# An adaLN block with linear attention and a token mixer on one core: row turns in F32R, last channels of phi(q) in pairs of tiles, two folded vectors, and a reordered beginning

## The chip, the core and the metric

The kernel runs on one core of one Trainium2 chip. The metric is device time in microseconds (us). Most executions of this kernel lie within 0.04 us of each other: three runs gave 437.96, 437.97 and 438.0. Engine names are those of the profile: PE is TensorE's products, PEld its weight loads, DVE is VectorE, ACT is ScalarE, POOL is GpSimd, SP is SyncE, which issues most of the DMAs.

## The reference

One sequence of S = 2048 tokens with D = 448 channels, H = 16 heads of 28, F = 1792. All inputs are float32.

```python
mod = (_silu(c) @ w_mod).reshape(c.shape[0], 6, 1, -1)
sa, ca, ga, sb, cb, gb = ...
h = _layernorm(x) * (1 + ca) + sa
x = x + ga * _A_ref(h, A_wqkv, A_wo)
h = _layernorm(x) * (1 + cb) + sb
x = x + gb * _B_ref(h, B_w1, B_b1, B_w2, B_b2)
```

`_A_ref` is linear attention: q, k and v from one projection, phi(t) = (t + 1 where t > 0, else exp(t)) + 1e-6, kv = phi(k)^T v summed over the tokens, and the output is phi(q) kv divided by phi(q) . sum(phi(k)) + 1e-6, times wo. `_B_ref` mixes tokens: gelu(h^T w1 + b1) w2 + b2, for each channel.

## The kernel before

A token tile is 128 tokens; there are NT = 16. A product in full float32 is made of F32R products: a number is split into a high half (an ACT copy to F32R) and a low half (a DVE subtraction), and hi*hi + hi*lo + lo*hi are added in PSUM. `bank(...)` is one of eight PSUM banks, `slot` and `tslot` are SBUF buffers, `moving` an F32R buffer of 448 columns. The kernel sets its own order: each engine runs its instructions in the order in which the lines call them, and waits where an operand or a buffer is not ready.

The 448 channels are three chunks of 128 and a last one of 64. The 64 channels of the last chunk share one product: high half in 64 partitions, low half in the other 64.

**The beginning** (lines 150 to 178 and 531 to 645). The loads go out one behind the other on SP's queue: weights of k (`load_qkv(1)`), the columns of w_mod that give 1 + ca (`load_first(1, ch)`) and those that give sa (`load_first(0, ch)`), the transposed tokens `load_xt(t)` and the tokens `load_x(t)`. `keep_warm(n)` issues n float32 products of 128 columns, each as two instructions, whose result nobody reads. `col_sum(j, ch)` (L220) gives a chunk of the modulation as a column on DVE; `w_high`, `w_low` and `w_row` scale and split the weights; `row_part(1, ch)` (L265, L267) adds up sa times the weights into `accb`, which `row_bias` (L277) sums with a product; `row_sum` (L274) sums the weights' columns; `row_out` (L281, L282) turns both into rows of `Wrow`. `a_split_high(t)` (L398) and `a_split_low(t)` (L402) split tile t of xt. `projects` and `project` (L419) make x times the weights of k (`kp`) or q (`qp`), and `close` (L426) adds mean and bias as one more product, for which the tile's mean and root must stand as rows in its low half.

Each tile's statistics come from ACT for tiles 0 and 1 (`a_stats_act`, L348 to L356) and from DVE for the others (`a_stats_dve`, L367 to L373); the power -0.5 is on POOL (`a_pow`, L339). Two tiles' statistics are put in columns (`a_rows`, L382 and L385), turned by one PE instruction to rows (`a_transpose`, L391; eight in all), and copied by ACT (`a_copy`, L394). `a_exp` (L433, L436) and `a_pk` (L441) make phi(k); `a_pk_parts` (L499, L501 or L503 and a DMA that adds, L504) splits it and adds it to one of two running sums, for tiles 2 to 12 with a DMA on POOL's queue that adds (L508). `a_norm`, `a_high` and `a_low` (L479 to L489) make and split the normalised tile, and `a_outer` (L525, L529) adds the tile's phi(k) x^T.

**The k loop** (lines 647 to 736) does tiles 4 to 15, with five tiles of q in between. In it and behind it, `mod_part`, `mod_split` and `mod_sum2` (L226 to L241) make modulation vectors 2, 3, 4 and 5: four chunks of 112 rows are weighted and added on DVE, split, and summed over the partitions by two products with ones.

**The phi(q) loop** (lines 932 to 1001) is a pipeline of steps i over the tiles; LAG = 5. In PE's order a step has `b_transpose(i)` (L820, three transposes of 128 columns, and L821, one of 64), `b_out(i - 1)` (L845, eleven products), a tile of q in the first steps, and from step 5 on twelve products of the mixer's first matrix for tile i - 5 (`step`, L895 to L897). DVE's order within a step is: a part of vector 5 in steps 13 to 16 (L226, L228), `b_res(i - 2)` (L854, the residual, which reads the bank of `b_out(i - 2)`), `b_prod(i + 1)` (L795), `b_norm1_a` (L864), `b_sum(i + 1)` (L799), `b_norm1_b` (L868), `b_low(i)` (L830), `b_recip(i + 1)` (L805), `b_low_last(i)` (L834), `b_scale(i + 1)` (L809, which writes the `pn` that the next step's transposes turn), and `b_low2(i - 4)` (L892). ACT starts a step with `b_high(i)` (L825, L826).

Behind it, to the end, come the rest of the mixer's first matrix (L895 to L897) and its second (L1109 to L1113).

## Time and profile before

| What | us |
|---|---|
| Median of three runs | 437.97 |
| The profiled execution: device time | 438.01 |
| Its span, first to last instruction | 436.3 |
| PE busy within the span | 429.2 |
| PE's share of the chain that ended last | 89% |
| DVE busy | 360.6 |
| ACT busy | 275.3 |
| POOL busy | 117.9 |

A row of the timeline is: start in us, duration in us, engine, line of the kernel, operation, what it writes and reads, shape, count, and in brackets how long the engine was idle before it and what ended that. Two products in a row on PE overlap: each starts about 0.2 us behind the one before and takes 0.36 to its modelled end, so the distance of the starts is what a product costs. A row of busy time by stretches is: the stretch, its length, then busy time and count for PE, PEld, DVE, ACT and POOL, the granted clock of PE, the DMA engines' share and GB/s. A row of groups is: line, engine, operation, shapes, count, then busy us and mean ns of one, then idle us before them and what ended it.

### The profile page before, as it was taken

To read this page: it belongs to the slowest core of one execution; us is meant where nothing else is said; L and a number is where in the kernel's file an instruction comes from. 1 tells how busy PE (TensorE), PEld (TensorE's weight loads), DVE (VectorE), ACT (ScalarE), POOL (GpSimd) and SP (SyncE) were. 2 spreads that over 40 slices of the span, in tenths; PEclk is the share of its full clock that TensorE was granted. 3 is DMA by queue.
4 is the path that set the end of the run, shared out by engine and by line. 5 is a ranking of instruction groups with operands and counts; after the bars stand their busy time and mean duration, and the time that the engine had idled before them with its cause. 6 is when DMAs were issued, how large, how long until landed. Compare 5 with 4: busy or idle time off the path is not lost.

```text
span 436.3 us, 7203 instructions
## 1 busy us (share of the span) xinstructions
PE 429.2 (98%) x2337; PEld 398.8 (91%) x2337; DVE 360.6 (83%) x809; ACT 275.3 (63%) x587; POOL 117.9 (27%) x200
## 2 busy tenths in 40 slices
PE   8899999999999999999999999999999999999996
PEld 8688899999899999999999999999999999999996
DVE  4899986689799999994679695829799988898894
ACT  5689867749657798886756263537464565645550
POOL 4335454100024477773300000010113131132010
PEclk9999999999999999999999999999999999999999
DMA  8997998465300036335417561587379977985430
GB/s 273 382 338 154 228 230 200 80 193 180 124 2 0 26 66 152 74 74 139 152 65 223 178 209 45 148 213 218 71 171 235 201 173 156 223 180 119 83 54 32
DMA packets 63941, 66.14 MB, mean 152 GB/s; under 512 B 4960, under 2 KB 55456, under 8 KB 63904
## 3 DMA queue, kind: packets, MB, share of 16 engines
q1 hardware_dynamic: 54832, 50.90, 37.6%
q0 software_dynamic: 8784, 14.32, 20.9%
q10 hardware_dynamic: 288, 0.46, 0.5%
q8 instruction: 18, 0.29, 0.3%
q14 instruction: 19, 0.16, 0.1%
HBM read 46.30 MB, written 7.34 MB: 123 GB/s over the span
## 4 chain that ended last, share of the span: by engine, by line
PE 89%; DVE 3%; DMA 2%; ACT 2%; POOL 1%; issue 1%; SPq 1%; DVEq 0%; ACTq 0%; POOLq 0%
PE y L1112 19%; PE up L897 10%; PE up L896 10%; PE up L895 10%; PE y L1113 9%; PE op L845 8%; PE qp L419 7%; PE cacc L525 6%; PE kp L419 3%; PE tq L820 1%; DMA wr<-in_qkv_dram 1%; DMA x<-in_A_x_dram 1%; PE qp L426 1%; PE kvb L776 1%; DVE st L367 1%
## 5 line engine op out<-in xcount | busy, mean ns | idle before, releaser
L896 PE MATMUL up<-h2l,ph 128*128 128x448 f32 x224 | 81.3, 363 | 0.0
L897 PE MATMUL up<-h2h,pl 128*128 128x448 f32 x224 | 81.2, 363 | 0.0
L895 PE MATMUL up<-h2h,ph 128*128 128x448 f32 x224 | 80.8, 361 | 0.0
L1067 POOL DMA_DIRECT2D a<-a x16 | 14.2, 959 | 138.0 <-DMA a<-in_B_w_dram 77.1
L896 PEld LDWEIGHTS up<-h2l,ph 128*128 128x128 f32 x224 | 42.0, 188 | 3.3 <-DVE h2l L892 0.3
L895 PEld LDWEIGHTS up<-h2h,ph 128*128 128x128 f32 x224 | 41.9, 187 | 3.0
L897 PEld LDWEIGHTS up<-h2h,pl 128*128 128x128 f32 x224 | 42.0, 188 | 2.5
L84 DVE TENSOR_TENSOR pl<-pr,ph 128x512 fp32r<-128x512 f32 x46 | 30.7, 685 | 4.2 <-ACT ph L83 3.3
L1118 ACT ACTIVATE cc<-y 128x448 f32<-128x448 f32 x24 | 13.0, 547 | 26.8 <-PE y L1113 26.8
L83 ACT ACTIVATE ph<-pr 128x512 fp32r<-128x512 f32 x46 | 27.6, 625 | 0.8 <-PE up L897 0.5
L1031 DVE TENSOR_TENSOR u<-u,mod 128x448 f32<-128x448 f32 x14 | 8.7, 621 | 21.6 <-ACT u L1030 21.4
L419 PE MATMUL kp<-wh,hh 128*128 128x448 f32 x64 | 24.4, 386 | 0.2 <-ACT rk L436 0.2
L845 PE MATMUL op<-wph,pth 128*128 128x448 f32 x64 | 24.5, 383 | 0.0
L1030 ACT ACTIVATE u<-up,b1c 128x448 f32<-128x448 f32 x14 | 8.8, 627 | 24.0 <-PE up L897 23.5
L1132 POOL DMA_DIRECT2D out_dram<-yt x14 | 12.7, 910 | 40.5 <-DVE yt L1123 31.1
L525 PE MATMUL cacc<-pkh,xh 128*128 128x448 f32 x64 | 23.6, 369 | 0.0
L419 PE MATMUL qp<-wh,hh 128*128 128x448 f32 x64 | 23.4, 366 | 0.0
L845 PE MATMUL op<-wpl,pth 128*128 128x448 f32 x64 | 23.1, 361 | 0.0
L802 POOL TENSOR_SCALAR den<-den 128x16 f32<-128x16 f32 x16 | 8.8, 549 | 43.6 <-DVE den L799 43.6
L525 PE MATMUL cacc<-pkl,xh 128*128 128x448 f32 x56 | 20.3, 362 | 0.0
L1073 DVE TENSOR_TENSOR a<-a,s 128x512 f32<-128x512 f32 (+1 forms) x32 | 18.5, 619 | 0.0
L1112 PE MATMUL y<-ub,a11h 128*128 128x448 f32 x56 | 18.2, 375 | 0.0
(233 smaller groups left out, 1362.3 us busy)
## 6 DMA issues: line engine op xcount, KB each, us to landing
pr<-in_B_w_dram SPq DMA_DIRECT2D x56, 256.0 KB, 3.0
a<-in_B_w_dram SPq DMA_DIRECT2D x32, 256.0 KB, 4.6
a<-in_B_w_dram SPq DMA_DIRECT2D x32, 192.0 KB, 4.6
xt<-in_xt_dram SPq DMA_DIRECT2D x16, 256.0 KB, 5.0
x<-in_A_x_dram SPq DMA_DIRECT2D x16, 224.0 KB, 5.0
wm<-in_B_wmod_dram SPq DMA_DIRECT2D x16, 196.0 KB, 4.9
out_dram<-x SPq DMA_DIRECT2D x14, 224.0 KB, 2.4
out_dram<-yt POOLq DMA_DIRECT2D x14, 224.0 KB, 5.5
```

The costliest lines, as they stand in the source:

```text
L83: nc.scalar.activation(hi, full, AF.Copy)
L84: nc.vector.tensor_sub(lo, full, hi.bitcast(F32))
L419: nc.tensor.matmul(pps[t, j][:, :D], a[:, ch * P:(ch + 1) * P], w, start=first, stop=False)
L525: nc.tensor.matmul(cacc[ch][:, :D], a[:, s], b, start=(t == 0 and i == 0), stop=(t == NT - 1 and i == len(todo) - 1))
L845: nc.tensor.matmul(opb[t][:, :D], a, b, start=(n == 0), stop=(n == len(todo) - 1))
L895: nc.tensor.matmul(ps[:, :D], hi[:, sl], mh, start=first, stop=False)
L896: nc.tensor.matmul(ps[:, :D], hi[:, sl], ml, start=False, stop=False)
L897: nc.tensor.matmul(ps[:, :D], lo[:, sl], mh, start=False, stop=last)
L1067: nc.gpsimd.dma_start(w, a, accum_op=ALU.add)
L1073: nc.vector.tensor_tensor(w, raw2[q, a][i], raw2[q, b][i], op=op)
L1112: nc.tensor.matmul(ps[:, :D], h[:, s], w, start=opens and r == 0, stop=False, skip_group_check=True)
L1113: nc.tensor.matmul(ps[:, :HD], l[:, s], wh, start=False, stop=closes and r == PAIRS - 1, skip_group_check=True)
```

## The change

Five parts. (1) `ident_r` is an F32R copy of the identity; `a_transpose` multiplies by it in F32R instead of a float32 transpose. (2) `mod_split` of vectors 2 and 5 (`FOLDED`) adds rows 64 to 111 to rows 0 to 47 on DVE, puts high and low halves into one buffer of 128 partitions, and `mod_sum2` sums these with one product. (3) In the phi(q) loop an even tile's last 64 channels are copied by ACT (`b_beside`) into the columns behind the next, odd tile's channels, and the odd tile's fourth transpose turns both; `b_high` and `b_low_last` do the last channels of both tiles in the odd step, and an even tile's last two products (`b_out_last`) move to the start of PE's step i + 2, ahead of `b_transpose`; `b_res` of that tile keeps its place. (4) The sums of phi(k) by DMA are gathered and issued behind the power of the next statistics (`sum_end`). (5) The beginning is reordered: x0 ahead of the four `load_first(0, ch)` and x1 in their middle; seven instead of four `keep_warm`; `col_sum(0, .)` and `row_part(1, .)` alternate in twos; the splits of tiles 3 to 6 move; two small operations of `a_stats_act` go from POOL to DVE.

```diff
--- before.py
+++ after.py
@@ -42,6 +42,7 @@
 WARM = 6
 POOL_LOW = (0, 2)
 PRE = 9
+FOLDED = (2, 5,)
 MID = 5
 NSLOT, NTOK = 74, 27
 LOAD2, SPLIT2 = 12, 4
@@ -97,6 +98,7 @@
                             pattern=[[0, 4], [-DH, 4], [0, DH]], channel_multiplier=1)
     nc.gpsimd.affine_select(out=m3, in_=m3, compare_op=ALU.is_ge, fill=0.0, base=DH - 1,
                             pattern=[[0, 4], [DH, 4], [0, DH]], channel_multiplier=-1)
+    ident_r = cst.tile([P, P], F32R, name="ident_r")
     cst.tile([P, 112], F32, name="space")
     mhalf = cst.tile([P, 2], F32, name="mhalf")
     nc.vector.memset(mhalf, -0.5)
@@ -158,10 +160,11 @@
         if ch == 1:
             load_xt(1)
     load_xt(2)
+    load_x(0)
     for ch in range(4):
+        if ch == 2:
+            load_x(1)
         load_first(0, ch)
-    load_x(0)
-    load_x(1)
     load_xt(3)
     load_xt(4)
     load_x(2)
@@ -228,16 +231,31 @@
             nc.vector.scalar_tensor_tensor(macc[j], wm[j, k], sc[:G, k:k + 1], macc[j], op0=ALU.mult, op1=ALU.add)
 
 
+    def halves(acc, new, name):
+        n = acc.shape[0] - 64
+        nc.vector.tensor_add(acc[:n], acc[:n], acc[64:])
+        both = moving(new, name)
+        nc.scalar.activation(both[:64], acc[:64], AF.Copy)
+
+        def low():
+            nc.vector.tensor_sub(both[64:], acc[:64], both[:64].bitcast(F32))
+        return both, low
+
     def mod_split(j):
         acc = macc.pop(j)
-        macc[j] = (moving(slot, f"mh{j}", parts=G), moving(slot, f"ml{j}", parts=G))
-        split(acc, *macc[j])
+        if j in FOLDED:
+            both, low = halves(acc, slot, f"mh{j}")
+            low()
+            macc[j] = (both,)
+        else:
+            macc[j] = (moving(slot, f"mh{j}", parts=G), moving(slot, f"ml{j}", parts=G))
+            split(acc, *macc[j])
 
     def mod_sum2(j):
         ps = bank(f"modp{j}")
-        hi, lo = macc.pop(j)
-        nc.tensor.matmul(ps[:, :D], ones_r[:G, :], hi, start=True, stop=False)
-        nc.tensor.matmul(ps[:, :D], ones_r[:G, :], lo, start=False, stop=True)
+        part = macc.pop(j)
+        for i, m in enumerate(part):
+            nc.tensor.matmul(ps[:, :D], ones_r[:m.shape[0], :], m, start=(i == 0), stop=(i == len(part) - 1))
         return ps
 
     Whi, Wlo, Wrow, rowb, accb = {}, {}, {}, {}, {}
@@ -350,8 +368,8 @@
             b_square(X[t], s3[:, 1:2], s3[:, 2:3], f"s{t}")
 
         def end():
-            nc.gpsimd.tensor_scalar_mul(g[:, :, 0:1], sm[:, :, 0:1], 1.0 / D)
-            nc.gpsimd.tensor_scalar(ve, sm[:, :, 2:3].to_broadcast([P, n, 2]), 1.0 / D, EPS,
+            nc.vector.tensor_scalar_mul(g[:, :, 0:1], sm[:, :, 0:1], 1.0 / D)
+            nc.vector.tensor_scalar(ve, sm[:, :, 2:3].to_broadcast([P, n, 2]), 1.0 / D, EPS,
                                     op0=ALU.mult, op1=ALU.add)
             a_pow(g, ve)
             groups[ts[0]] = g
@@ -388,7 +406,7 @@
     def a_transpose(t):
         ps = bank(f"rw{t}")
         tps[t], tps[t + 1] = ps[:ROWS - 64, :P], ps[64:ROWS, :P]
-        nc.tensor.transpose(ps[:ROWS, :P], rowst[t // 2 % RING][:, :ROWS].bitcast(F32), ident)
+        nc.tensor.matmul(ps[:ROWS, :P], rowst[t // 2 % RING][:, :ROWS], ident_r, start=True, stop=True)
 
     def a_copy(t):
         nc.scalar.activation(heads[t][1][64:ROWS, 384:], tps.pop(t), AF.Copy)
@@ -505,11 +523,17 @@
         if t < 2:
             pksum.append(pk)
         elif t in SUM_DMA:
-            nc.gpsimd.dma_start(pksum[t % 2], pk, accum_op=ALU.add)
+            late_sum.append((pksum[t % 2], pk))
         else:
             nc.vector.tensor_add(pksum[1], pksum[1], pk)
         pks[t] = (hi, lo)
 
+
+    late_sum = []
+
+    def sum_end():
+        while late_sum:
+            nc.gpsimd.dma_start(*late_sum.pop(0), accum_op=ALU.add)
 
     cacc = []
 
@@ -529,7 +553,7 @@
                 nc.tensor.matmul(cacc[ch][:, :D], xh[:, ch * P:(ch + 1) * P], kl, start=False, stop=False)
 
     spread()
-    keep_warm(4)
+    keep_warm(7)
     nc.scalar.activation(sel_s, sel_f, AF.Copy)
     col_sum(1, 0)
     a_split(0)
@@ -559,20 +583,21 @@
     w_row(1)
     act01, end01 = a_stats_act((0, 1))
     act01(0)
-    for ch in range(4):
+    nc.scalar.activation(ident_r, ident, AF.Copy)
+    for ch in (0, 2):
         col_sum(0, ch)
+        col_sum(0, ch + 1)
+        row_part(1, ch)
+        row_part(1, ch + 1)
     row_sum(1)
-    a_split_high(3)
     act01(1)
     end01()
-    row_part(1, 0)
-    a_split_low(3)
-    for ch in (1, 2, 3):
-        row_part(1, ch)
-    a_split(4)
+    a_split(3)
     projects(in_turn(3)[:4], 1, "kp")
     row_bias(1)
     projects(in_turn(3)[4:], 1, "kp")
+    a_split_high(4)
+    a_split_high(5)
     low = a_rows(0)
     first23, second23, end23 = a_stats_dve((2, 3))
     first23(0)
@@ -581,8 +606,8 @@
     second23(0)
     second23(1)
     end23()
-    a_split_high(5)
     row_out(1)
+    a_split_low(4)
     a_transpose(0)
     a_copy(0)
     a_copy(1)
@@ -596,6 +621,7 @@
     load_mod(2)
     load_xt(10)
     load_x(10)
+    a_split_high(6)
     a_exp(0, kps[0])
     a_high(0)
     low = a_rows(2)
@@ -619,7 +645,7 @@
     a_pk(1, kps[1])
     low = a_rows(4)
     low()
-    a_split(6)
+    a_split_low(6)
     a_transpose(4)
     a_exp(2, kps[2])
     a_pk(2, kps[2])
@@ -641,6 +667,7 @@
     low = a_rows(6)
     a_pk_parts(2)
     low()
+    sum_end()
     a_split(7)
     wo_sb = []
     late = [t for t in range(NT) if t not in Q_EARLY.values()]
@@ -701,6 +728,7 @@
         if pair:
             second(1)
             end()
+        sum_end()
         if 4 <= t < 8:
             w_high(0, t - 4)
             if t == 7:
@@ -788,7 +816,7 @@
     H2h, H2l = [None] * NT, [None] * NT
     pns, phs, ys, opb, sums, nms, nm2s, rss, vss = {}, {}, {}, {}, {}, {}, {}, {}, {}
 
-    dens, prods = {}, {}
+    dens, prods, lasts = {}, {}, {}
 
     def b_prod(t):
         prods[t] = tslot(f"pd{t}")
@@ -805,8 +833,8 @@
         nc.vector.reciprocal(dens[t], dens[t])
 
     def b_scale(t):
-        pn = tslot(f"pn{t}")
-        nc.vector.scalar_tensor_tensor(pn.rearrange("p (h d) -> p h d", d=DH),
+        pn = pns.pop(t, None) or tslot(f"pn{t}", w=512)
+        nc.vector.scalar_tensor_tensor(pn[:, :D].rearrange("p (h d) -> p h d", d=DH),
                                        pq[t].rearrange("p (h d) -> p h d", d=DH), 1e-6,
                                        dens.pop(t).unsqueeze(2).to_broadcast([P, H, DH]),
                                        op0=ALU.add, op1=ALU.mult)
@@ -816,33 +844,47 @@
     def b_transpose(t):
         pn = pns.pop(t)
         tps[t] = bank(f"tq{t}")
-        for ch in range(3):
+        if t % 2 == 0:
+            lasts[t] = pn
+        for ch in range(3 + t % 2):
             nc.tensor.transpose(tps[t][:, ch * P:(ch + 1) * P], pn[:, ch * P:(ch + 1) * P], ident)
-        nc.tensor.transpose(tps[t][:64, 384:], pn[:, 384:D], ident)
+
+    def b_beside(t):
+        pns[t + 1] = tslot(f"pn{t + 1}", w=512)
+        nc.scalar.activation(pns[t + 1][:, D:], lasts.pop(t)[:, 384:D], AF.Copy)
 
     def b_high(t):
         phs[t] = (slot(f"pth{t}", 512, F32R), slot(f"ptl{t}", 384, F32R))
         nc.scalar.activation(phs[t][0][:, :384], tps[t][:, :384], AF.Copy)
-        nc.scalar.activation(phs[t][0][:64, 384:], tps[t][:64, 384:], AF.Copy)
+        if t % 2:
+            for i, s in ((t, slice(0, 64)), (t - 1, slice(64, P))):
+                nc.scalar.activation(phs[i][0][s, 384:], tps[t][s, 384:], AF.Copy)
 
     def b_low(t):
         hi, lo = phs[t]
         nc.vector.tensor_sub(lo, tps[t][:, :384], hi[:, :384].bitcast(F32))
 
     def b_low_last(t):
-        ps, hi = tps.pop(t), phs[t][0]
-        nc.vector.tensor_sub(hi[64:, 384:], ps[:64, 384:], hi[:64, 384:].bitcast(F32))
+        ps = tps.pop(t)
+        if t % 2:
+            for i, s, o in ((t - 1, slice(64, P), slice(0, 64)), (t, slice(0, 64), slice(64, P))):
+                hi = phs[i][0]
+                nc.vector.tensor_sub(hi[o, 384:], ps[s, 384:], hi[s, 384:].bitcast(F32))
 
     def b_out(t):
-        ph, pl = phs.pop(t)
+        ph, pl = phs[t]
         opb[t] = bank(f"op{t}")
-        todo = []
         for ch in range(3):
             s = slice(ch * P, (ch + 1) * P)
-            todo += [(ph[:, s], Wph[ch]), (ph[:, s], Wpl[ch]), (pl[:, s], Wph[ch])]
-        todo += [(ph[:, 384:], Wph[3]), (ph[:, 384:], Wpl[3])]
-        for n, (a, b) in enumerate(todo):
-            nc.tensor.matmul(opb[t][:, :D], a, b, start=(n == 0), stop=(n == len(todo) - 1))
+            for n, (a, b) in enumerate(((ph[:, s], Wph[ch]), (ph[:, s], Wpl[ch]), (pl[:, s], Wph[ch]))):
+                nc.tensor.matmul(opb[t][:, :D], a, b, start=(ch == n == 0), stop=False)
+        if t % 2:
+            b_out_last(t)
+
+    def b_out_last(t):
+        ph = phs.pop(t)[0]
+        for b in (Wph, Wpl):
+            nc.tensor.matmul(opb[t][:, :D], ph[:, 384:], b[3], start=False, stop=(b is Wpl))
 
     def b_sums(i):
         if i not in vss:
@@ -936,6 +978,8 @@
             mod_part(5, i - NT + 3)
         if i == NT:
             mod_split(5)
+        if i % 2 == 0 and 0 < i <= NT:
+            b_out_last(i - 2)
         if i < NT:
             b_transpose(i)
         if 0 <= i - 1 < NT:
@@ -958,6 +1002,8 @@
             mod_out(5, mp)
         if i < NT:
             b_high(i)
+            if i % 2 == 0:
+                b_beside(i)
         a_exp_q(nq)
         scale, res, norm1, norm2 = i + 1 < NT, 0 <= i - 2 < NT, 0 <= i - 3 < NT, 0 <= i - 4 < NT
         if res and i < NT + 1:
```

## The prediction

> **What bounds the kernel now.** I read the page's head and its chain of work first, then busy time by stretches, then TensorE's (PE's) own timeline where a stretch was not full, and last the VectorE (DVE) timeline beside it.
>
> ```profile
> span 436.3 us, 7203 instructions
> PE 429.2 (98%) x2337; PEld 398.8 (91%) x2337; DVE 360.6 (83%) x809; ACT 275.3 (63%) x587; POOL 117.9 (27%) x200
> PE 89%; DVE 3%; DMA 2%; ACT 2%; POOL 1%; issue 1%; SPq 1%; DVEq 0%; ACTq 0%; POOLq 0%
> ...
> 15.00:20.00 5.00, 3.38 (x16) 2.32 (x15) 3.44 (x7) 3.72 (x11) 2.15 (x3) 1.00 1.05 382
> 200.00:300.00 100.00, 100.00 (x501) 93.43 (x500) 68.61 (x161) 52.11 (x114) 7.82 (x17) 1.00 0.51 151
> ```
>
> PE holds 89% of the chain. From 200 to 300 us it starts 501 products of 448 columns in 100 us, one every 0.20 us. So time is to be had in two ways: fewer PE instructions, each worth its pitch, or less waiting where PE waits, which is before 45 us:
>
> ```profile
> 6.33 2.08 PE L184 MATMUL warm<-ones 128*128 128x128 f32 x8
> 8.06 0.72 PE L419 MATMUL kp<-wh,hh 128*128 128x448 f32 x1
> ...
> 8.95 0.57 PE L419 MATMUL kp<-wl,hh 128*128 128x448 f32 x1
> 9.32 0.57 PE L419 MATMUL kp<-wh,hh 128*128 128x448 f32 x1
> ...
> 18.93 0.99 PE L277 MATMUL rowb<-accb,sel_b 128*98 128x448 f32 x2 [1.62 <-DVE accb L267]
> ...
> 22.35 0.65 PE L426 MATMUL kp<-wrow,hl 98*128 98x448 f32 x2 [0.49 <-DVE wrow L282]
> ...
> 29.47 0.47 PE L419 MATMUL kp<-wh,hh 128*128 128x448 f32 x1 [0.19 <-ACT rk L436]
> ...
> 43.56 0.32 PE L391 MATMUL rw<-ident,rowst 128*98 128x128 f32 x1 [0.17 <-DVE rowst L385]
> ```
>
> Four waits, 1.62 + 0.49 + 0.19 + 0.17 = 2.47 us; and up to 9.3 us products start 0.37 apart, so PE is near half its later pace there. The sum below is made against the profiled execution's own 438.01 us (span 436.3 and 1.7 around it); the median of the runs, 437.97, stands 0.04 beside it.
>
> **The first operations.** Who was late?
>
> ```profile
> 13.88 0.58 ACT L348 ACTIVATE junk<-x 128x448 f32<-128x448 f32 x1 [1.75 <-DMA x<-in_A_x_dram]
> 15.50 0.62 ACT L398 ACTIVATE hh<-xt 128x512 fp32r<-128x512 f32 x1
> ...
> 14.46 0.44 DVE L265 TENSOR_SCALAR accb<-wr,col 128x448 f32<-128x448 f32 x1
> 16.15 0.69 DVE L402 TENSOR_TENSOR hl<-xt,hh 128x512 fp32r<-128x512 f32 x1 [1.25 <-ACT hh L398]
> 16.76 2.12 DVE L267 SCALAR_TENSOR_TENSOR accb<-wr,col,accb 128x448 f32<-128x448 f32 x3
> 19.82 0.17 DVE L382 CAST rowst<-mv 128x8 fp32r<-128x8 f32 x1 [0.34 <-POOL mv L339]
> 21.58 0.63 DVE L282 TENSOR_TENSOR wrow<-rowb,wrow 2x448 fp32r<-2x448 f32 x1
> ...
> 18.29 1.50 POOL L339 TENSOR_TENSOR mv<-ve,roots 128x4 f32<-128x4 f32 x1
> ```
>
> ScalarE (ACT) sits 1.75 us for the first x tile, so the third tile's high half is late, and DVE, which has its split in the queue ahead of accb's last three parts, sits 1.25 us. In the new order x0 is loaded ahead of four 224 KB tiles. At 382 GB/s one takes 0.6 us, so x0 lands at 13.88 - 4 x 0.6 = 11.5, before ACT is free (12.13). The loads of the first vector land up to 1.2 us later than now, still ahead of the products that read them, since row parts now stand between these. DVE then runs accb's parts without what now lies between 14.90 (the end of L265) and 16.76: done at 18.88 - 1.86 = 17.0. ACT does both tiles' statistics, 1.62 us each (13.88 to 15.50), and the new 128x128 copy of the identity (about 0.3) by 12.13 + 3.24 + 0.3 = 15.7. The two small operations taken from GpSimd (POOL) stand on DVE behind accb, at about 0.2 each (the cast's row has 0.17): 17.4. The split of tile 3 (0.69) fits in front of the power's end, for the power of 1.50 ends at 19.0 instead of 19.79; the cast, the chain behind it and L282 come 0.8 us sooner, and the two closing products at 22.35 - 0.75 = 21.6.
>
> Three more warming products cost (8.06 - 6.33)/4 = 0.43 us each, 1.3 us at most, ahead of the first real product. PE is done with what it has at 18.93 - 1.62 = 17.3 now, so at 18.6 at the latest, and has then at most 2.9 us of work (the bias 0.99, nine products 1.8, one turn 0.1) before the closing products: 21.5, in front of their 21.6. What hides the 1.3 us is the wait for DVE; without it they cost all of it.
>
> What is late next is DVE. The low half of tile 4 (0.69) moves behind L282 and 0.4 us came over from POOL, so the normalisations after it start only 0.1 to 0.3 sooner; the earlier exponent, tile 6's high half taken ahead of it, and the gapless DVE queue up to 35 us keep about 0.7. Then comes the row turn at 43.56:
>
> ```profile
> 40.05 1.24 POOL L508 DMA_DIRECT2D pk<-pk  x1
> 40.73 1.97 POOL L339 TENSOR_TENSOR mv<-ve,roots 128x4 f32<-128x4 f32 x1
> ```
>
> The power waits behind a sum's DMA on POOL's queue. With the sums put behind the power it starts some 0.7 us sooner, and the cast and the turn with it. The sums are wanted only when the last tile is added, so their delay is covered. Bounds for the whole stretch: 2.47 if every wait goes, 0.3 if only the normalisations' gain is kept. I take **1.05**: the 0.75 of the closing products and most of the two short waits, nearest to the rows that chain through DVE.
>
> **Row turns in F32R.**
>
> ```profile
> 54.90 0.27 PE L391 MATMUL rw<-ident,rowst 128*98 128x128 f32 x1
> ...
> 55.21 0.37 PE L419 MATMUL kp<-wl,hh 128*128 128x448 f32 x1
> ```
>
> From the turn's start to the second product behind it is 0.31; less 0.20 for the first, a turn costs 0.11. As an F32R product of 128 columns it costs 0.20 x 128/448 = 0.057 by the wide products, or, if F32R runs at plain F32's rate, a warming product's 0.43 at the later pace, 0.43 x 0.20/0.37 = 0.23. I take 0.08, between the turn's own row and the wide products, because the weights of the next product must still be loaded in its shadow. Four of the eight turns lie behind the head: **-0.1** (bounds -0.2 and +0.5). The Trainium skill, "TensorE: Matmul & The Clock Gate", Back-to-back issue gap, gives 81 ns for a pair of weight load and 128-column product in a stream, not 128 columns' share of a wide one; by it the four would save 0.12, by the wide products' row 0.21.
>
> **Folded vectors.** Each loses one 448-column product: **-0.4**. Each gains one DVE addition (under 0.7); the first stands two steps ahead of its use, the second in step 16, where PE has two groups of products before it asks.
>
> **Last channels in pairs.** An odd tile's fourth transpose now turns both tiles' 64 channels.
>
> ```profile
> 152.93 0.49 PE L820 MATMUL tq<-ident,pn 128*128 128x128 f32 x3
> 153.25 0.27 PE L821 MATMUL tq<-ident,pn 128*64 128x128 f32 x1
> ...
> 153.57 0.36 PE L845 MATMUL op<-wpl,pth 128*128 128x448 f32 x1
> 157.97 0.49 PE L820 MATMUL tq<-ident,pn 128*128 128x128 f32 x3
> ```
>
> Three transposes take 153.25 - 152.93 = 0.32, and the 64-wide one 153.57 - 0.20 - 153.25 = 0.12: a transpose costs 0.107 whatever its width, and eight fewer give **-0.86**. The number of output products stays. ACT gains eight copies and DVE nothing:
>
> ```profile
> L825 ACT ACTIVATE pth<-tq 128x384 fp32r<-128x384 f32 x9 | 4.4, 490 | 4.4 <-PE tq L821 4.3
> L826 ACT ACTIVATE pth<-tq 64x128 fp32r<-64x128 f32 x9 | 2.3, 259 | 0.0
> ```
>
> A copy of 0.26 in every other step lies under ACT's wait of 4.4/9 = 0.49 us in each.
>
> The price is order. An even tile's last two products now open PE's step two later, and the residual (L854), which heads DVE's queue in that step, waits for them; behind it stand the next tile's scale (L809) and so the next transposes.
>
> ```profile
> 157.52 0.62 DVE L854 SCALAR_TENSOR_TENSOR x<-op,x 128x448 f32<-128x448 f32 x1
> ...
> 161.07 0.28 DVE L834 TENSOR_TENSOR pth<-tq,pth 64x128 fp32r<-64x128 f32 x1
> 161.38 0.62 DVE L809 SCALAR_TENSOR_TENSOR pn<-pq,den 128x448 f32<-128x448 f32 x1
> ...
> 162.46 0.62 DVE L854 SCALAR_TENSOR_TENSOR x<-op,x 128x448 f32<-128x448 f32 x1
> ```
>
> DVE works without a gap: 4.94 us a step, 4.49 from L854 to the end of L809, against PE's 157.97 - 152.93 = 5.04. Today L854 starts 0.45 ahead of PE's step. Call T the start of the opening products of an even step; L854 can start at T + 0.2 + 0.36 + 0.05 = T + 0.61. An even step has no L834 now (0.31 with its gap) and an odd one has two. So L809 ends at T + 0.61 + 4.18 = 4.8 in the even step; PE asks at 25 x 0.20 + 0.33 = 5.33, its weight load 0.2 earlier: 0.3 to spare. In the odd step L809 ends at 4.8 + 0.45 + 4.8 = 10.05, and the load wants it at 9.97 + 0.2 = 10.17, behind the next opening products: 0.1 to spare. DVE's pair takes 9.88, PE's 10.08 - 0.11 = 9.97, so PE still sets the pace, barely. "VectorE: DVE Perf Modes" of the Trainium skill, Two Vector instructions with no wait between them, holds an instruction that starts in another quadrant than the last until all earlier ones are done, which speaks against the pair of L834; the 0.03 us gap ahead of L809 agrees. Had the second L834 overlapped the first as other operations do, 0.1 more would be spare.
>
> Three steps near the end have one DVE operation more:
>
> ```profile
> 182.23 0.45 DVE L226 TENSOR_SCALAR acc<-wm,sc 112x448 f32<-112x448 f32 x1
> 187.53 0.68 DVE L228 SCALAR_TENSOR_TENSOR acc<-wm,sc,acc 112x448 f32<-112x448 f32 x1
> 188.25 0.49 PE L820 MATMUL tq<-ident,pn 128*128 128x128 f32 x3
> 192.00 0.62 DVE L809 SCALAR_TENSOR_TENSOR pn<-pq,den 128x448 f32<-128x448 f32 x1
> 193.30 0.49 PE L820 MATMUL tq<-ident,pn 128*128 128x128 f32 x3
> ```
>
> Now they eat a lead of DVE (at 193.30 still 0.68 after L809's end). Without it, the 0.45 of step 13 exceeds the 0.1 to spare by about 0.3, and step 14's 0.6 exceeds an even step's 0.3 by another 0.3: **+0.6**. Bounds: nothing, if a lead remains, and 1.2 if the 0.1 to spare is missing in each of six other pairs too.
>
> **Sum.** 438.0 - 1.05 - 0.1 - 0.4 - 0.86 + 0.6 = **436.2 us**. Behind 200 us nothing changes; PE is full there, so what is gained is kept.
>
> **Rivals.** *The opening products bind DVE* (slower than before): the residual held back at 0.21 behind PE's transposes instead of 0.45 ahead, 0.66 us a pair, is paid by PE in each of the seven pairs, 4.6 us instead of 0.6: 438.0 - 2.4 + 4.6 = 440.2. It decides once DVE's pair with its hold takes longer than PE's 9.97; against it stands 9.88, for it that the margin is 0.1. *The lead remains*: the hold is shorter, and no step stalls: 435.6. *The head gives nothing*: the operations moved to DVE eat the 0.75: 438.0 - 1.36 + 0.6 = 437.2; for it, that DVE shows no gap between 24 and 35 us. *F32R of 128 columns at F32's rate*: eight turns lose 0.12 each: 438.0 - 1.05 + 1.0 - 0.4 - 0.86 + 0.6 = 437.3; for it and against it no row speaks.
>
> **How the numbers follow.** Forecast 0.55, the lead remains 0.15, the head gives nothing 0.13, F32R slow 0.08, DVE bound 0.09. The forecast's own range is 435.6 to 436.9 (head 0.6 to 1.4, stalls 0.3 to 1). The low end 435.0 is a head of 1.6, no stall, full F32R gain; the high end 437.9 takes in the empty head, slow F32R, and 1.2 of stalls with a head of 0.3 (437.5). Less than 2 in 10 lie outside, mostly DVE bound. 0.2%, 0.88 us, is about what a measurement of this kernel tells from no change: faster (under 437.1) is the forecast, the lead and 0.04 of the head's rival, 0.74; the rest of that rival and slow F32R lie within, 0.17; slower 0.09.
>
> **What would show it.** Right: the wait for accb gone and the closing products near 21.6; the turn of tile 8 without a wait; 56 transposes instead of 64 at 0.107; L854 in even steps starting just after the opening products; short PE waits for L809 at two transposes near 190. Wrong: a PE wait at the transposes of every second step, or a turn that costs over 0.11.

## The result, and the profile after

Six runs of the changed kernel gave a median of **436.02 us** (435.86 to 436.36); six of the kernel before on the same chip 437.99 (437.96 to 438.39). The ratio is 0.9955, with a 95% interval of 0.9942 to 0.9968. The forecast was 436.2, in a range of 435.0 to 437.9. The profiled execution is the slowest of the six: 436.36, span 434.7, so 1.65 less than the profiled execution before.

The head of the page and its chain of work:

```profile
span 434.7 us, 7209 instructions
PE 429.1 (99%) x2333; PEld 398.1 (92%) x2333; DVE 362.3 (83%) x813; ACT 279.3 (64%) x596; POOL 118.6 (27%) x198
...
PE 92%; DVE 4%; DMA 2%; issue 1%; POOL 0%; ACT 0%; SPq 0%; DVEq 0%
```

PE is busy for as long as before in a span shorter by 1.6: what went is waiting. What PE saved in products (the folded vectors and eight transposes) it spends on the three more warming pairs, 3.34 us of warming products in place of 2.08. The view of PE's waits (what it waited for, us in total, times, longest) lists three now:

```profile
PE warm L187 <- DVE roots L107: 1.1, 1, 1.1
PE kp L444 <- DVE wrow L300: 0.7, 1, 0.7
PE tq L850 <- DVE pn L837: 0.2, 1, 0.2
```

The first stands at the very beginning and was there before the change too. The waits for accb, for the row turn of tile 8 and for ACT at 29.47 are gone; one at the transposes is new. PE's timeline shows where (L295 is the bias product, L444 the closing one, L409 the row turn, L887 the opening products, L850 the transposes):

```profile
6.32 3.34 PE L187 MATMUL warm<-ones 128*128 128x128 f32 x14
9.33 0.54 PE L437 MATMUL kp<-wh,hh 128*128 128x448 f32 x1
...
17.72 0.91 PE L295 MATMUL rowb<-accb,sel_b 128*98 128x448 f32 x2
...
21.48 0.65 PE L444 MATMUL kp<-wrow,hl 98*128 98x448 f32 x2 [0.75 <-DVE wrow L300]
...
42.40 0.22 PE L409 MATMUL rw<-ident_r,rowst 128*98 128x128 f32 x1
...
53.66 0.23 PE L409 MATMUL rw<-ident_r,rowst 128*98 128x128 f32 x1
...
53.97 0.36 PE L437 MATMUL kp<-wl,hh 128*128 128x448 f32 x1
...
155.93 0.36 PE L887 MATMUL op<-wpl,pth 128*128 128x448 f32 x1
156.46 0.52 PE L850 MATMUL tq<-ident,pn 128*128 128x128 f32 x3 [0.16 <-DVE pn L837]
...
186.26 0.36 PE L887 MATMUL op<-wpl,pth 128*128 128x448 f32 x1
186.63 0.52 PE L850 MATMUL tq<-ident,pn 128*128 128x128 f32 x3
...
191.40 0.36 PE L939 MATMUL up<-h2h,pl 128*128 128x448 f32 x1
191.85 0.63 PE L850 MATMUL tq<-ident,pn 128*128 128x128 f32 x4
```

Matching each product with the same product of the kernel before, its start has moved as follows (after less before; a minus is earlier):

| At about (us) | Move | What lies in between |
|---|---|---|
| 9.3 | +1.28 | three more warming pairs |
| 18 | -1.21 | no wait for accb |
| 22 to 30 | -0.7 to -1.1 | closing products, no wait for ACT |
| 42 | -0.83 | part of the lead lost again |
| 46 | -1.24 | no wait at the turn of tile 8 |
| 58 to 72 | -1.17 | four row turns in F32R |
| 80 to 112 | -1.40 | first folded vector, -0.22 |
| 150 | -1.85 | four pairs of tiles |
| 160 | -1.60 | transposes of tile 8 late, +0.33, and one fewer, -0.1 |
| 180 | -1.80 | two more pairs |
| 190, 195 | -1.70, -1.43 | tile 14 late, about 0.2, and one fewer, -0.1; tile 15 late, 0.27 |
| 212 to the end | -1.65 | second folded vector, -0.22 |

The transposes of tiles 8, 14 and 15 would be due 0.20 behind the product ahead of them, at 156.13, 186.46 and 191.60; the rows have 156.46, 186.63 and 191.85. The view of waits counts only the 0.16 us of tile 8 in which PE stood idle.

Now the engines that PE used to wait for. DVE:

```profile
15.87 1.39 DVE L285 SCALAR_TENSOR_TENSOR accb<-wr,col,accb 128x448 f32<-128x448 f32 x2
17.18 0.16 DVE L371 TENSOR_SCALAR mv<-as 128x2 f32<-128x2 f32 x1
17.25 0.17 DVE L372 TENSOR_SCALAR ve<-as 128x4 f32<-128x4 f32 x1
...
18.95 0.17 DVE L400 CAST rowst<-mv 128x8 fp32r<-128x8 f32 x1 [0.94 <-POOL mv L357]
...
20.70 0.63 DVE L300 TENSOR_TENSOR wrow<-rowb,wrow 2x448 fp32r<-2x448 f32 x1
...
146.33 0.62 DVE L896 SCALAR_TENSOR_TENSOR x<-op,x 128x448 f32<-128x448 f32 x1 [0.95 <-PE op L887]
...
150.96 0.62 DVE L471 SCALAR_TENSOR_TENSOR pq<-eq,rq 128x448 f32<-128x448 f32 x1
...
155.68 0.63 DVE L837 SCALAR_TENSOR_TENSOR pn<-pq,den 128x448 f32<-128x448 f32 x1
...
156.76 0.62 DVE L896 SCALAR_TENSOR_TENSOR x<-op,x 128x448 f32<-128x448 f32 x1
```

accb is ready at 15.87 + 1.39 = 17.26 in place of 18.88, and the small operations follow it without a gap. In phi(q) DVE stands idle for 0.95 us before the residual L896 at 146.33, which waits for the opening products (they start at T = 145.72, so this is T + 0.61, as the prediction has it); L837, which the transposes need, ends at 156.31. POOL:

```profile
17.50 1.42 POOL L357 TENSOR_TENSOR mv<-ve,roots 128x4 f32<-128x4 f32 x1 [3.75 <-DVE ve L372]
...
39.89 1.56 POOL L357 TENSOR_TENSOR mv<-ve,roots 128x4 f32<-128x4 f32 x1 [0.34 <-DVE ve L391]
41.26 0.90 POOL L536 DMA_DIRECT2D pk<-pk  x1
```

The power now stands ahead of the sum's DMA, and it waits for DVE and no longer for POOL's own queue.

### The profile page after: what moved, and what is told of

The parts are those of the page before. It is cut to its first block, busy times and chain, and to the rows that moved or that the text cites. A ratio compares the mean times of both kernels' runs of the same rounds, so it can differ in the third digit from the quotient of the medians.

```text
span 434.7 us, 7209 instructions
## 1 busy us (share of the span) xinstructions
PE 429.1 (99%) x2333; PEld 398.1 (92%) x2333; DVE 362.3 (83%) x813; ACT 279.3 (64%) x596; POOL 118.6 (27%) x198
## 4 chain that ended last, share of the span: by engine, by line
PE 92%; DVE 4%; DMA 2%; issue 1%; POOL 0%; ACT 0%; SPq 0%; DVEq 0%
PE y L1158 19%; PE up L937 10%; PE up L939 10%; PE up L938 10%; PE y L1159 9%; PE cacc L549 8%; PE qp L437 7%; PE op L880 6%; PE kp L437 6%; PE tq L850 1%; PE op L887 1%; DMA wr<-in_qkv_dram 1%; DMA xt<-in_xt_dram 1%; PE kp L444 1%; PE qp L444 1%; PE kvb L804 1%
## 5 line engine op out<-in xcount | busy, mean ns | idle before, releaser
L1077 DVE TENSOR_TENSOR u<-u,mod 128x448 f32<-128x448 f32 x14 | 8.7, 622 | 21.6 <-ACT u L1076 21.4
L880 PE MATMUL op<-wph,pth 128*128 128x448 f32 x48 | 18.7, 390 | 0.0
L84 ACT ACTIVATE s2h<-s 128x512 fp32r<-128x512 f32 (+1 forms) x16 | 8.4, 571 | 15.5 <-DVE s L1119 15.5
```

Source lines behind the costliest of these rows:

```text
L84: nc.scalar.activation(hi, full, AF.Copy)
L880: nc.tensor.matmul(opb[t][:, :D], a, b, start=(ch == n == 0), stop=False)
```

## The experiments

Each time is a median, with the lowest and the highest run in brackets. The ratio is to runs of the kernel before on the same chip (medians 438.09, 438.08 and 437.95 in the three sets), with its 95% interval. These runs of the kernel before span 437.64 to 438.81, far more than the 0.04 of its first three. "Ahead", "later" and moves with a sign are starts of matched products against the first profile of the changed kernel.

**The last channels in pairs, undone** (the rest as changed):

```diff
-        for ch in range(3 + t % 2):
+        for ch in range(3):
...
+        nc.tensor.transpose(tps[t][:64, 384:], pn[:, 384:D], ident)
...
-        if i % 2 == 0 and 0 < i <= NT:
-            b_out_last(i - 2)
```

> The changed kernel with the phi(q) loop of before: 64 transposes, an even tile's last two products with the others, no copy beside. Theory (the pairs save 0.86 us of transposes and pay 0.7 us of PE waits for L809's scale, 0.24 at the transposes of tile 8, 0.20 at tile 14 and 0.27 at tile 15): no PE wait at any transpose, and the time within 0.3 us of the changed kernel's 436.0, so 1.7 to 2.1 us under the kernel before. Rival (the waits in the profile are paid back behind the loop, the pairs keep their 0.86): 436.9, 1.1 under the kernel before.

Measured: 435.91 (435.62 to 435.98), ratio 0.9947 (0.9932 to 0.9961). Its view of PE's waits has, behind the warming, one row:

```profile
PE kp L444 <- DVE wrow L300: 0.3, 1, 0.3
```

There is no wait at a transpose. The theory holds, but for its 0.24 at tile 8: that is the stall of 0.33 less the tile's own saved transpose. The beginning of this run lies 0.38 ahead (see the last section). From there it falls back 0.46 by 150 us, over four pairs of tiles; the stall that it lacks at tile 8 puts it 0.18 ahead; two more pairs take that away (+0.02 at 182); and without the stalls of tiles 14 and 15 it is at -0.35 from 198 us on. So the pairs save their eight transposes and pay that back in waits: nothing is left of them.

**The first operations in the old order**, with the sums still behind the power:

```diff
-    keep_warm(7)
+    keep_warm(4)
...
-    for ch in (0, 2):
-        col_sum(0, ch)
-        col_sum(0, ch + 1)
-        row_part(1, ch)
-        row_part(1, ch + 1)
+    for ch in range(4):
+        col_sum(0, ch)
```

with the old places of the loads of x0 and x1, of the splits of tiles 3 to 6, and of the two small operations.

> The changed kernel with the beginning of before: load order, four warming products, the order of column sums, row parts and splits, and the two small statistics operations on POOL; the F32R turns, pairs, folds and the sums behind the power stay. Theory (the beginning is worth 1.24 us at 46 us, of which 0.35 to 0.4 come from the sums behind the power at the turn of tile 8): PE waits for accb 1.6 us and for L282's row about 0.5 us again, product starts at 46 us are 0.7 to 0.9 later than in the changed kernel, time 436.8 (436.6 to 437.0). Rival (the beginning gives all of the 1.24 alone): 437.25. Second rival (DVE is the bound to 46 us whatever stands in front): 436.0 to 436.2.

Measured: 437.63 (437.25 to 438.49), ratio 0.9992 (0.9982 to 1.0001), above all three forecasts. Starts lie 1.22 later from 52 us to the end, and 1.64 later than those of the repeat below; the medians differ by 1.6, with a wide spread. The waits of before are back (lines are one lower in this kernel):

```profile
PE rowb L294 <- DVE accb L284: 1.7, 1, 1.7
...
PE kp L443 <- DVE wrow L299: 0.5, 1, 0.5
PE kp L436 <- ACT rk L453: 0.2, 1, 0.2
```

That is the whole gain of the beginning, though the sums' new place is still in: what is left against the kernel before, 438.09 - 437.63 = 0.46, is about what the folded vectors give (below). So the two parts do not add. With PE late, the turn of tile 8 does not wait, and the sums' place gives nothing.

**The sums issued early again**:

```diff
-            late_sum.append((pksum[t % 2], pk))
+            nc.gpsimd.dma_start(pksum[t % 2], pk, accum_op=ALU.add)
```

> The accumulating DMA of each pair of k tiles is issued in its old place on POOL's queue, ahead of the next power, and not behind it; all else is the changed kernel's. Theory as the prediction had it: the power of the rows from tile 8 on starts up to 0.7 later, the turn of tile 8 waits 0.17 to 0.4 again, and the time is 436.2 to 436.4. Rival, from the run with the whole beginning undone, in which that turn did not wait although its sums were issued early: nothing moves, 436.0.

The rival's premise was false: in the run just told the sums stood behind the power too. Measured: 436.4 (436.34 to 436.53), ratio 0.9961 (0.9948 to 0.9973), as the theory has it. Its POOL timeline:

```profile
38.85 1.24 POOL L526 DMA_DIRECT2D pk<-pk  x1
39.53 1.97 POOL L357 TENSOR_TENSOR mv<-ve,roots 128x4 f32<-128x4 f32 x1
```

This run is 0.35 ahead up to 42 us and is level from the turn of tile 8 to the end. The power stands right behind the sum and ends at 39.53 + 1.97 = 41.50, although everything ahead of it is 0.35 earlier; on the changed kernel it ends at 39.89 + 1.56 = 41.45. The sums' place is worth 0.38, by moves and by medians (436.40 less 436.02), once the rest of the beginning is earlier.

**Four warming pairs in place of seven** (`keep_warm(4)`):

> Four pairs of warming products ahead of the first real product, as before the change, in place of seven; all else is the changed kernel's. Theory (the three more are hidden by PE's wait for L300's row at the closing products): first real product about 1.3 earlier, the wait at the closing products longer by as much, closing products within 0.1 of 21.5, time within 0.1 of 436.0. Rival (the clock comes to full speed later in real products, so these take longer and the warming pays for itself): 0.2 to 0.6 slower. Second rival (the warming costs what it takes, 1.3): 434.7.

Measured: 435.85 (435.57 to 436.11), ratio 0.9948 (0.9936 to 0.9961). PE's timeline:

```profile
5.97 1.16 PE L187 MATMUL warm<-ones 128*128 128x128 f32 x8
7.53 0.47 PE L437 MATMUL kp<-wh,hh 128*128 128x448 f32 x1 [0.40 <-ACT wh L265]
...
19.06 0.30 PE L409 MATMUL rw<-ident_r,rowst 128*98 128x128 f32 x1 [0.23 <-DVE rowst L403]
...
20.77 0.65 PE L444 MATMUL kp<-wrow,hl 98*128 98x448 f32 x2 [0.75 <-DVE wrow L300]
```

The wait for L300's row is the same 0.75, so it is DVE's chain that sets the closing products. PE has also got a wait of 0.40 for the first weights, which takes up part of the time saved. The medians' 0.17 is inside the spread of either kernel. The closing products are not within the 0.1 that the theory gave: the beginning itself moves by more from execution to execution, as the next run shows.

**The changed kernel once more**, no edit:

> The changed kernel once more, nothing edited. In the profiles so far the three more warming pairs either took as long as the first four (14 products in 3.34, first real product at 9.33) or half as long (14 in 1.83, first real product at 7.5 to 7.9), and the closing products stood at 21.5 in the one and at 21.1 in the other. Theory (this varies between executions of one kernel and is no effect of the edits): the time within 435.8 to 436.5; if this execution has the faster beginning, its starts lie 0.3 to 0.5 ahead of the first profile's from 25 us to the end. Rival (the edits of the other kernels brought it): the same beginning as in the first profile, all starts within 0.1.

Measured: 435.97 (435.93 to 436.01), ratio 0.9955 (0.9942 to 0.9967).

```profile
3.86 1.19 PE L210 MATMUL scr<-ident,sc 112*128 112x112 f32 x8
...
5.29 1.83 PE L187 MATMUL warm<-ones 128*128 128x128 f32 x14
6.87 0.45 PE L437 MATMUL kp<-wh,hh 128*128 128x448 f32 x1
...
21.11 0.65 PE L444 MATMUL kp<-wrow,hl 98*128 98x448 f32 x2 [0.75 <-DVE wrow L300]
```

The closing products come 0.37 earlier than in the first profile, and all starts behind 60 us 0.42 earlier to the end, in the same kernel. The theory holds. So a move of up to 0.4 that comes from the beginning of a single execution proves nothing; moves inside one trace are not touched by this. The stalls at tiles 8, 14 and 15 are here as they were: 0.33, 0.18 and 0.25.

**Row turns as float32 transposes**:

```diff
-        nc.tensor.matmul(ps[:ROWS, :P], rowst[t // 2 % RING][:, :ROWS], ident_r, start=True, stop=True)
+        nc.tensor.transpose(ps[:ROWS, :P], rowst[t // 2 % RING][:, :ROWS].bitcast(F32), ident)
```

> The changed kernel with the eight row turns as float32 transposes. Theory, from the changed kernel's trace (turn to the second product behind it 0.31 us in both): a turn costs 0.11 either way, the time is that of the changed kernel within 0.1 us, and the starts of products at 80 us stand within 0.1 us. Rival, as forecast (0.03 saved in each): 0.1 to 0.2 us slower than the changed kernel.

Measured: 436.05 (435.97 to 436.32), ratio 0.995 (0.9934 to 0.9967).

```profile
53.52 0.27 PE L409 MATMUL rw<-ident,rowst 128*98 128x128 f32 x1
...
53.84 0.36 PE L437 MATMUL kp<-wl,hh 128*128 128x448 f32 x1
```

From the turn to the second product behind it are 0.32 us, against 0.31 in F32R above: 0.12 and 0.11 a turn. The form changes nothing, as the theory has it.

**No folded vectors** (`FOLDED = ()`):

> The two vectors that the change folds are multiplied by two wide products each again, as before the change; all else is the changed kernel's. Theory (each fold saves one 448-column product at the end of its vector's chain, 0.20 to 0.22, and its one DVE addition lies beside other work): PE's later starts fall behind by 0.2 at the first vector and by 0.2 more at the second, 436.4 to 436.5 against the changed kernel's 436.0. Rival (the addition takes from DVE in phi(q) what the product gives): the same 0.2 up to the second vector, then nothing or a gain, since tile 15's wait of 0.27 gets shorter without it: 436.0 to 436.2.

Measured: 436.4 (436.22 to 436.63), ratio 0.9962 (0.9948 to 0.9975). Starts lie 0.44 ahead to 65 us, 0.23 ahead from 90 to 199, and 0.02 from 211 on: 0.21 lost at each vector, and nothing at tile 15. The theory holds.

**The residual of an even step later in DVE's queue**:

```diff
-        if res and i < NT + 1:
+        wait = i % 2 == 0 and i < NT
+        if res and i < NT + 1 and not wait:
             b_res(i - 2)
         if scale:
             b_prod(i + 1)
...
+        if wait and norm1:
+            b_norm1_a(i - 3)
+        if res and wait:
+            b_res(i - 2)
...
-        if norm1:
+        if norm1 and not wait:
             b_norm1_a(i - 3)
```

> The changed kernel, with an even step's residual (L896) moved in DVE's queue behind the next tile's product with the sum (L823) and the first normalisation (L906), 1.14 us later in the queue, so that what heads DVE's queue no longer waits for the opening products. Theory (the waits at tiles 8, 14 and 15 come from the lead that DVE loses to the residual): no DVE wait on PE in even steps from 6 on, no PE wait at the transposes of tiles 8, 14 and 15, 0.7 us gained: 435.3. Rival (DVE's amount of work, not its order, makes it late; its step of 4.94 stays): at most 0.2 gained, 435.8 to 436.0. Other side (the mean on POOL and the square on ACT behind the later residual come late and hold ACT's queue): slower, 436.5 or more.

Measured: 435.09 (434.78 to 435.26), ratio 0.9928 (0.9913 to 0.9943).

```profile
155.47 0.37 PE L887 MATMUL op<-wpl,pth 128*128 128x448 f32 x1
155.67 0.49 PE L850 MATMUL tq<-ident,pn 128*128 128x128 f32 x3
```

The transposes follow 0.20 behind the opening product, with no wait here nor at tiles 14 and 15; the move goes from -0.47 at 150 to -1.28 at 198, so 0.81 in the loop. The three stalls hang on the residual's place in DVE's queue. One sign of the theory did not come: in step 6 DVE still waits 0.33 for the opening products, at 145.86; no later transpose is late for it.

**The two small operations back on POOL**:

```diff
-            nc.vector.tensor_scalar_mul(g[:, :, 0:1], sm[:, :, 0:1], 1.0 / D)
-            nc.vector.tensor_scalar(ve, sm[:, :, 2:3].to_broadcast([P, n, 2]), 1.0 / D, EPS,
+            nc.gpsimd.tensor_scalar_mul(g[:, :, 0:1], sm[:, :, 0:1], 1.0 / D)
+            nc.gpsimd.tensor_scalar(ve, sm[:, :, 2:3].to_broadcast([P, n, 2]), 1.0 / D, EPS,
```

> The two small operations on the sums of the rows' statistics go back from DVE to POOL; all else is the changed kernel's. Theory (in the changed kernel they stand behind accb on DVE and so the first power starts at 17.50, though ACT's sums are there by about 15.9): on POOL they end by about 16.6, the power by 18.1 instead of 18.92, the cast and the closing products come 0.7 sooner, and 0.3 to 0.7 of it stays: 435.3 to 435.7. Rival (POOL takes them at 0.23 and 0.42, and the later ends, which have POOL's DMA issues and powers before them, are late instead): closing products sooner, but waits of 0.2 or more at row turns behind 25 us, and the time 436.0 or above.

Measured: 435.3 (435.01 to 436.07), ratio 0.9937 (0.9925 to 0.995). POOL's timeline:

```profile
15.70 0.69 POOL L372 TENSOR_SCALAR ve<-as 128x4 f32<-128x4 f32 x1 [0.79 <-ACT junk L345]
16.47 1.49 POOL L357 TENSOR_TENSOR mv<-ve,roots 128x4 f32<-128x4 f32 x1
```

The power starts at 16.47 instead of 17.50, the cast on DVE stands at 18.00 instead of 18.95, and PE's closing products at 20.53. Against the repeat (21.11) that is 0.58, and its starts are 1.0 ahead of the first profile's against the repeat's 0.42: the same 0.58 to the end. The move to DVE, part of the change, cost more than half a microsecond.

**Both, then two more steps.** First the two last edits together; then with `row_out(1)` (L300) ahead of `second23(0)` as well; then all that with `keep_warm(4)`.

> Two edits together: the residual of an even step stands later in DVE's queue, and the two small operations on the statistics' sums are on POOL. Theory (one acts before 45 us, the other in phi(q), and PE is full between): the gains add, 0.95 and 0.7 below the changed kernel's 436.0, 434.3 to 434.5. Rival (DVE, with what it gains at the beginning, is not what phi(q) waits for, but the earlier beginning brings another engine or load to bind): 434.7 to 435.0.

> As the kernel with both edits, and L300's row of wrow stands on DVE ahead of the second and last operations of the statistics of tiles 2 and 3. Theory (with the sums on POOL the closing products wait 0.49 for that row alone; moved ahead it ends at about 19.9, and ACT's copies of the turned rows at 20.0 are next): closing products 0.4 earlier, 433.9 to 434.1. Rival (the power of tiles 2 and 3 comes 0.6 later, and the turn of tile 2 at about 23 waits for it): the same as with both edits, or later by up to 0.3.

> As the last, with four pairs of warming products in place of seven. Theory (with the row early nothing hides the three pairs any longer, and PE itself arrives late at the closing products): 0.3 to 0.7 faster than the last, 433.3 to 433.7. Rival (PE only comes to full pace later, and the turned rows come when they come): within 0.15 of the last.

Measured: 434.17 (434.02 to 434.36), 434.13 (434.04 to 434.34) and 434.41 (434.25 to 434.61); ratios 0.9914 (0.99 to 0.9927), 0.9912 (0.9899 to 0.9926) and 0.9919 (0.9906 to 0.9933). The gains of the two edits add, and a little more: 435.97 - 434.17 = 1.80, against 0.88 and 0.67 for each alone. In the loop it is the 0.81 of the late residual again (-1.32 at 150 us, -2.13 at 198); the 0.25 over the sum arose before 45 us and is within what the beginning varies. With 434.17 this kernel is faster than the one before and the changed one. The next step has its rival right. PE's timeline:

```profile
20.00 0.65 PE L444 MATMUL kp<-wrow,hl 98*128 98x448 f32 x2
...
22.30 0.30 PE L409 MATMUL rw<-ident_r,rowst 128*98 128x128 f32 x1 [0.23 <-DVE rowst L403]
```

The closing products no longer wait, and the turn of tile 2 does, as the rival has it. Fewer warming pairs still bring nothing (starts 0.03 earlier, the median 0.28 later), and the theory, that nothing hides the three pairs any longer, falls: PE stands 0.4 us each at the first weights' high and low halves instead, and the closing products come only 0.1 sooner.

## Why the prediction was right, step by step

- **The beginning, -1.05.** Measured -1.24 at 46 us in the first profile, in which a load came some 0.3 late (last section), and 0.4 more in the repeat; undoing it cost 1.6 by the medians. The reasons held: accb at 17.26 (predicted 17.0), the power's end at 18.92 (19.0), closing products at 21.48 (21.6), no wait at tile 8. The power's delay behind the sum was shown by putting it back: 0.38. So the term was too small, by 0.2 to 0.6.
- **"What hides the 1.3 us is the wait for DVE; without it they cost all of it."** The first half was shown: with three pairs fewer the wait of 0.75 stays and the time does not fall. The second half failed: in the last two runs the closing products do not wait for DVE, and taking the three pairs out still brings nothing.
- **The small operations "behind accb" on DVE.** Their times were right, but the prediction did not ask what they would have done on POOL. There the second of them starts at 15.70, when ACT has its sums, while on DVE both stand behind accb, which ends at 17.26: the largest thing that was overlooked, 0.6 us.
- **Row turns, -0.1.** Failed: 0. The step that failed is "I take 0.08": the turn keeps its 0.11, so the lower bound, a share of a wide product by columns (0.057), does not hold for a narrow product in this stream. The Trainium skill, "TensorE: Matmul & The Clock Gate", Back-to-back issue gap, gives 81 ns for such a pair; here the two forms measured 0.11 and 0.12, and the measurement decides.
- **Folded products, -0.4.** 0.22 and 0.22 in the first comparison, 0.21 each when undone.
- **Eight transposes, -0.86.** About as priced. Six are seen free of stalls, 0.65 together (-1.40 to -1.85, -1.60 to -1.80); the others lie at stalls. From 112 to 199 us the net of savings and stalls is -0.03, and the stalls are 0.8, so the savings are 0.83.
- **DVE's lateness, +0.6.** 0.8, and not only in the places given. Tiles 14 and 15 have 0.2 and 0.27, as argued; the 0.33 at tile 8 was not foreseen. The step that failed is DVE's pair of "9.88": until 151 us DVE also has L471, the last operation of phi(q) of a later tile, in each step, another 0.54 (150.96 to its successor at 151.50). With it the pair from 146.33 to 156.76 is 10.43, without a gap, over PE's 9.97; L837 ends at 156.31, 0.5 later than the sum in the prediction has it, and its 0.1 to spare is gone. Steps before 143 us have L471 too, but there PE has products of q to do as well and is not that fast. The trace of the kernel before had shown this operation (there L453), just ahead of the stretch that was counted, and DVE's order as listed ahead of the prediction leaves it out:

```profile
152.05 0.62 DVE L453 SCALAR_TENSOR_TENSOR pq<-eq,rq 128x448 f32<-128x448 f32 x1
```

  No run moved this operation alone: that it makes the difference between tile 8 and the tiles behind it is read from the rows. That the stalls need the residual's place was shown.
- **The rivals.** The lost time of every pair (440.2) did not come: between tiles 8 and 14 no pair stalls. A beginning that gives nothing, and F32R at plain float32's rate, are out. No stall at all, the case of "the lead remains", came only with the late residual.

That the sum came within 0.2 of the median is partly luck, errors of opposite sign: 0.2 to 0.6 too little gain at the beginning, 0.1 too much at the turns, 0.2 too little for the stalls.

## What to carry to other kernels

When PE saves work by pairing steps, ask what heads the other engine's queue in the step that waits for the pair, and put that operation behind those that the next step of PE needs: here one moved operation was worth as much as the whole saving. When a small operation is moved from a slow engine to a fast one, compare not their durations but when each queue gets to it. And count an engine's operations in every step of a loop, not in the steady ones alone.

## What was not expected of the hardware

The first microseconds of one and the same kernel differ. In the first profile the 14 warming products took 3.34, in the repeat 1.83; in the run with `row_out(1)` moved the eight products ahead of them were slow (2.02, in the repeat 1.19) and these fast (1.83). The granted clock does not show it: in both stretches (granted clock the third figure from the right) it is 1.00. First profile, then the repeat, busy time from 6 to 8 us:

```profile
6.00:8.00 2.00, 2.00 (x10) 1.99 (x11) 1.31 (x5) 0.84 (x2) 1.27 (x1) 1.00 1.00 381
```

```profile
6.00:8.00 2.00, 1.82 (x13) 1.52 (x13) 1.32 (x5) 1.58 (x3) 0.99 (x1) 1.00 1.02 368
```

The Trainium skill, "TensorE: Matmul & The Clock Gate", What's actually happening, says that PE starts at half rate and that the window which ends this runs freely, so that the point varies from run to run; the factor of about two and the varying point agree with these rows. It is not this pace that moves the closing products. In the run without pairs PE was as slow as in the first profile (first real product at 9.33 in both), and DVE's first column sum (L223) started at the same time; yet its third did not wait for a load. First profile, then the run without pairs:

```profile
6.49 0.62 DVE L223 SCALAR_TENSOR_TENSOR wt<-wt,scr 128x449 f32<-128x449 f32 x1 [2.78 <-PE scr L212]
...
8.82 0.62 DVE L223 SCALAR_TENSOR_TENSOR wt<-wt,scr 128x449 f32<-128x449 f32 x1 [0.28 <-DMA wt<-in_first_dram]
```

```profile
6.50 0.62 DVE L223 SCALAR_TENSOR_TENSOR wt<-wt,scr 128x449 f32<-128x449 f32 x1 [2.79 <-PE scr L212]
...
8.51 0.62 DVE L223 SCALAR_TENSOR_TENSOR wt<-wt,scr 128x449 f32<-128x449 f32 x1
```

The 0.31 between them is still there at L300 (20.70 and 20.39) and at the closing products (21.48 and 21.17). In the repeat, where PE was fast, the first column sum starts at 5.46, and the third waits 0.84 for its load, to 8.49. So some 0.3 of the varying 0.4 is the landing of one load; the kernel before had its third column sum at 8.49 too, so the first profile shows the change's beginning some 0.3 too small.
